# Turning q and k by halves, the order of a chunk's products, and seven PSUM banks dealt out anew, in a retention and feed-forward kernel

## Chip, cores and metric

One core of one Trainium2 chip. The metric is the device time of one execution in microseconds (us), as the median of several; lower is better.

## The reference

Retention (8 batches, 8 heads, 576 tokens, head size 64), then a feed-forward layer over all 4608 tokens with a squared ReLU. All in fp32.

```python
scores = scale * np.matmul(q, k.transpose(0, 1, 3, 2))
Dmat = np.where(rel >= 0, gamma[:, None, None] ** rel[None, :, :], 0.0)
attn = np.matmul(scores * Dmat, v)            # (B, H, S, D)
x = attn.transpose(0, 2, 1, 3).reshape(B * S, H * D)
h = np.maximum(x @ w_in, 0.0)                 # 512 -> 2048
return h * h @ w_out                          # 2048 -> 512
```

## The kernel before

Retention runs in 40 chunks (32 of 128 tokens, 8 of 64). One pass of the loop below, a *visit*, takes a chunk through one part of its work. Feed-forward steps of earlier tokens stand between the parts, so that TensorE has something to do while VectorE and ScalarE prepare the next part. The steps of block 0 (512 tokens) are plain products, L511 in the profile; from block 1 on a step is one of seven products of a Strassen scheme, L539. The second matrix of the layer comes last, L722.

For a chunk TensorE does this, in the profile's lines:

- *turn* of k and of q, L342: transposes by an identity matrix, since the scores need the head dimension on the partitions. ScalarE copies k out (L347), VectorE copies q out and applies a decay (L345).
- *scores*, L375: 64x64 products, read by VectorE with a mask into `ret` (L378).
- *a*, *b*, *c*, L392, L398 and L430: the retention output `x_ps` and the running state `u_ps`, all 64x64 products.

```python
ps_f = ctx.enter_context(tc.tile_pool(name="ps_f", bufs=4, space=PS))   # feed-forward
ps_a = first.enter_context(tc.tile_pool(name="ps_a", bufs=1, space=PS)) # turns
ps_x = first.enter_context(tc.tile_pool(name="ps_x", bufs=1, space=PS)) # x and scores, 2 banks
ps_u = first.enter_context(tc.tile_pool(name="ps_u", bufs=1, space=PS))
# ... cut ...
def turn(i, name):
    cs, c0 = chunks[i][3], chunks[i][2]
    src = loaded[i][name == "kT"]
    pool, tag = (ps_f, "f") if i < 6 else (ps_a, "a")
    p = pool.tile([128, HP, C], F32, tag=tag, name=f"{name}_ps")
    for hp in range(HP):
        nc.tensor.transpose(p[:, hp, :cs], src[:cs, 2 * hp:2 * hp + 2, :], ident[:cs, :cs])
    # ... cut: copy out by VectorE (q) or ScalarE (k) ...
# ... cut ...
for i in range(N_CH + 2):
    visit(i)                      # takes the two x banks
    if i >= 2:
        retain_a(i - 2)
    if i < N_CH:
        turn(i, "kT")
    # ... cut ...
    ffn(i - 2)                    # feed-forward steps that are due
    if i >= 2:
        retain_b(i - 2)
    if 1 <= i <= N_CH:
        scores(i - 1)
    if i < N_CH:
        turn(i, "qT")
    # ... cut ...
    ffn(i - 2)
    if i >= 2:
        # ... cut: steps that must come first ...
        retain_c(i - 2)
        convert(2 if i < 6 else 1)   # rounding of weights on VectorE
        ffn(i - 2)
    # ... cut ...
    if i + 2 < N_CH:
        load(i + 2)
```

## Time and profile before

| | |
|---|---|
| median of 3 | 1058.22 us (1057.21 to 1058.37) |
| TensorE busy in the profiled run | 996.0 us, 95% of the span of 1053.8 us |
| VectorE busy | 748.5 us, 71% |
| first feed-forward product | 55.4 us |
| first product of the last stage | 651.3 us |

What TensorE waits for, from its list of waits in the kernel before (us in total, times, longest):

```profile
PE kT_ps L342 <- DMA k_ld<-in_k_dram: 19.0, 6, 7.0
PE h_b L539 <- DVE room L475: 11.0, 3, 8.7
PE x_ps L392 <- ACT room L451: 8.3, 10, 1.2
PE x_ps L392 <- DVE ret L378: 6.8, 4, 4.6
PE x_ps L392 <- ACT w L451: 4.3, 4, 2.2
```

The first line is the start, which waits for loads of k. The second is feed-forward waiting for sums of its inputs on VectorE. The two `ACT` lines with L451 are waits for ScalarE's copy of the last chunk's output.

### The profile page before, as it was taken

What the parts mean: (1) busy time and instruction counts of PE and PEld (TensorE: products, weight loads), DVE (VectorE), ACT (ScalarE), POOL (GpSimd) and SP (SyncE); (2) the same over time, 40 slices, a digit from 0 to 9 for tenths busy, and PEclk for the clock granted to TensorE, in tenths of its full rate; (3) what the DMA queues carried; (4) which work ended last, traced back from release to release, by engine and by line L of the source; (5) the groups of instructions that cost most, each with busy time, mean ns of one, the idle gap of its engine ahead of it and who ended that gap; (6) DMA issues with size and microseconds to landing.
All of it is one profiled execution on the core that took longest, in us unless ns stands there. A gap on an engine that the chain in (4) does not pass through costs nothing.

```text
span 1053.8 us, 23361 instructions
## 1 busy us (share of the span) xinstructions
PE 996.0 (95%) x10120; PEld 876.6 (83%) x10120; DVE 748.5 (71%) x1414; ACT 184.7 (18%) x436; POOL 78.5 (7%) x82
## 2 busy tenths in 40 slices
PE   4699796999999999999999999899999999999998
PEld 3555455888888788888888888899999999999998
DVE  2377657776787878888887668667676677767775
ACT  2344321211122121221221100000000000000000
POOL 1111000111011010121110100000000000000000
PEclk9599898999999999999999999999999999999999
DMA  9969363744677788858956797954636546365351
GB/s 216 206 136 225 96 166 131 224 152 141 150 236 248 205 225 246 246 166 241 265 143 234 277 405 307 360 194 155 240 141 237 194 150 240 140 243 203 135 200 41
DMA packets 176342, 215.04 MB, mean 204 GB/s; under 512 B 115568, under 2 KB 124784, under 8 KB 167280
## 3 DMA queue, kind: packets, MB, share of 16 engines
q1 hardware_dynamic: 176240, 213.56, 64.5%
q8 instruction: 79, 1.29, 0.5%
q14 instruction: 23, 0.19, 0.1%
HBM read 125.19 MB, written 88.34 MB: 203 GB/s over the span
## 4 chain that ended last, share of the span: by engine, by line
PE 87%; DVE 5%; DMA 5%; ACT 1%; SPq 1%; issue 1%; DVEq 0%; ACTq 0%
PE h_b L539 16%; PE o_b L722 15%; PE h_c L539 10%; PE o_c L722 10%; PE o_a L722 10%; PE h_a L539 10%; PE h_ps L511 5%; DMA k_ld<-in_k_dram 3%; PE x_ps L392 3%; PE kT_ps L342 2%; PE x_ps L430 2%; PE qT_ps L342 2%; PE x_ps L375 1%; DMA a<-g_dram 1%; PE u_ps L398 1%
## 5 line engine op out<-in xcount | busy, mean ns | idle before, releaser
L539 PE MATMUL h_b<-room,w 128*128 128x256 f32 x736 | 177.4, 384 | 11.1 <-DVE room L475 11.0
L539 PEld LDWEIGHTS h_b<-room,w 128*128 128x128 f32 x736 | 138.0, 191 | 30.9 <-DVE room L475 12.0
L722 PE MATMUL o_b<-w,room 128*128 128x128 f32 x1168 | 144.5, 275 | 0.2 <-DVE room L694 0.2
L722 PEld LDWEIGHTS o_b<-w,room 128*128 128x128 f32 x1168 | 137.2, 192 | 0.5 <-DVE room L694 0.4
L722 PE MATMUL o_c<-w,room 128*128 128x128 f32 x1008 | 123.0, 275 | 0.0
L722 PEld LDWEIGHTS o_c<-w,room 128*128 128x128 f32 x1008 | 117.7, 192 | 0.0
L539 PE MATMUL h_c<-room,w 128*128 128x256 f32 x480 | 115.1, 383 | 0.0
L539 PE MATMUL h_a<-room,w 128*128 128x256 f32 x448 | 107.1, 382 | 0.0
L539 PEld LDWEIGHTS h_c<-room,w 128*128 128x128 f32 x480 | 90.2, 191 | 12.3
L539 PEld LDWEIGHTS h_a<-room,w 128*128 128x128 f32 x448 | 83.6, 190 | 11.8 <-issue 0.5
L722 PE MATMUL o_a<-w,a 128*128 128x128 f32 x688 | 85.9, 275 | 2.7 <-DMA a<-g_dram 2.7
L722 PEld LDWEIGHTS o_a<-w,a 128*128 128x128 f32 x688 | 81.3, 192 | 2.9 <-issue 2.9
L392 PEld LDWEIGHTS x_ps<-ret,v_ld 64*64 64x64 f32 x1152 | 44.5, 146 | 44.0 <-issue 33.3
L392 PE MATMUL x_ps<-ret,v_ld 64*64 64x64 f32 x1152 | 54.6, 238 | 20.0 <-ACT room L451 8.3
L546 DVE SCALAR_TENSOR_TENSOR room<-room 128x512 f32<-128x512 f32 x96 | 69.3, 722 | 3.3
L556 POOL TENSOR_TENSOR room<-room 128x512 f32<-128x512 f32 x32 | 34.6, 1081 | 471.2 <-ACT room L555 416.1
L733 ACT COPY r<-o_a 128x128 f32<-128x128 f32 x54 | 14.4, 266 | 276.9 <-PE o_a L722 236.1
L511 PE MATMUL h_ps<-room,w 128*128 128x512 f32 x128 | 60.2, 614 | 0.0
L558 DVE TENSOR_TENSOR room<-h_b,room 128x512 f32<-128x512 f32 x32 | 22.1, 691 | 46.5 <-PE h_b L539 46.5
L380 POOL TENSOR_TENSOR v_ld<-v_ld,dv 128x512 f32<-128x512 f32 (+1 forms) x40 | 43.5, 1090 | 97.7 <-DMA v_ld<-in_v_dram 87.0
L378 DVE TENSOR_TENSOR ret<-x_ps,msk 128x512 f32<-128x512 f32 (+1 forms) x40 | 27.4, 685 | 32.0 <-PE x_ps L375 26.5
L398 PE MATMUL u_ps<-v_ld,k_ld 64*64 64x64 f32 x1024 | 47.5, 237 | 0.0
(92 smaller groups left out, 1348.5 us busy)
## 6 DMA issues: line engine op xcount, KB each, us to landing
g_dram<-room SPq DMA_DIRECT2D x36, 1792.0 KB, 7.3
a<-g_dram SPq DMA_DIRECT2D x43, 1024.0 KB, 6.4
room<-g_dram SPq DMA_DIRECT2D x20, 1024.0 KB, 5.6
w<-w_dram SPq DMA_DIRECT2D x7, 1792.0 KB, 11.4
out_dram<-room SPq DMA_DIRECT2D x18, 512.0 KB, 3.3
q_ld<-in_q_dram SPq DMA_DIRECT2D x32, 256.0 KB, 5.8
k_ld<-in_k_dram SPq DMA_DIRECT2D x32, 256.0 KB, 6.4
v_ld<-in_v_dram SPq DMA_DIRECT2D x32, 256.0 KB, 6.8
```

Source lines behind the costliest of these rows:

```text
L342: nc.tensor.transpose(p[:, hp, :cs], src[:cs, 2 * hp:2 * hp + 2, :], ident[:cs, :cs])
L378: nc.vector.tensor_tensor(r[:cs], sc[:cs], msk[:cs].to_broadcast([cs, 2, HP, CH]), op=ALU.mult)
L380: nc.gpsimd.tensor_tensor(vs[:cs], vs[:cs], dv[:cs, :, ci:ci + 1].to_broadcast([cs, H, D]), op=ALU.mult)
L392: own.append(lambda g=g, e=e, b=b, head=head: nc.tensor.matmul(x_at(g, e, b, h), lhsT=s["vs"][rows(h), head, :], rhs=s["ret"][rows(h), e, ...
L398: grow.append(lambda hp=hp, e=e, head=head: nc.tensor.matmul(u_ps[0][rows(e), hp, :], lhsT=loaded[i][1][rows(1 - h), head, :], rhs=s["vs"] ...
L430: nc.tensor.matmul(x_at(g, e, b, h), lhsT=u[rows(e), 2 * b + g, :], rhs=s["qT"][rows(e), 2 * b + g, CH * h:CH * h + CH], start=clears(b, e ...
L511: nc.tensor.matmul(p.rearrange("p h t -> p (h t)"), lhsT=w[:, c, :], rhs=xT[0][:, c, :], start=(c == 0), stop=(c == N_DM - 1))
L539: nc.tensor.matmul(p[:, mm, :], lhsT=w[:, c, :], rhs=xs[n][right][:, c, :], start=(j in OPENS and mm == 0 and c == 0), stop=(j in CLOSES a ...
L546: nc.vector.scalar_tensor_tensor(t, t, 0.0, t, op0=ALU.max, op1=ALU.mult)
L556: nc.gpsimd.tensor_tensor(g["A11"], g["A11"], g["A11"], op=ALU.mult)
L558: nc.vector.tensor_tensor(g["A22"], p, p15, op=ALU.add)
L722: nc.tensor.matmul(p, lhsT=s["lefts"][left][:, m, :], rhs=w_out[j][:, m, WO_SLOT[right], :], start=(i in OPENS and m == 0), stop=(i in CLO ...
```

## The change

Its intent: make the transposes cheaper by running them in the two row halves of the array side by side, get q and k turned a visit earlier (one visit less of pipeline at the start), load three chunks ahead rather than two, and find the banks for it: turns and scores share two, x has two of its own, u has one, feed-forward keeps three of its four.

```diff
-    ps_f = ctx.enter_context(tc.tile_pool(name="ps_f", bufs=4, space=PS))
+    ps_f = ctx.enter_context(tc.tile_pool(name="ps_f", bufs=3, space=PS))
-    ps_a = first.enter_context(tc.tile_pool(name="ps_a", bufs=1, space=PS))
+    ps_t = first.enter_context(tc.tile_pool(name="ps_t", bufs=1, space=PS))
-    load(0)
-    load(1)
+    for i in range(3):
+        load(i)
 ... (old turn removed) ...
+    def turn(i):
+        cs, c0 = chunks[i][3], chunks[i][2]
+        n_h = cs // CH
+        p = ps_t.tile([128, 2, 512], F32, tag="t", name="t_ps").rearrange("p h (j d t) -> p h j d t", j=2, d=HP)
+        for j in (1, 0):
+            for hp in range(HP):
+                for h in range(n_h):
+                    nc.tensor.transpose(p[:, h, j, hp, :], loaded[i][j][rows(h), 2 * hp:2 * hp + 2, :],
+                                        ident[rows(h), rows(h)])
 ... (copies out by halves; kT in one buffer instead of two) ...
-        sc = xp[0][:, :, 256:].rearrange("p e (h t) -> p e h t", h=HP)
+        sc = ps_t.tile([128, 2, 512], F32, tag="t", name="sc_ps")[:, :, 0:256].rearrange("p e (h t) -> p e h t", h=HP)
 ... (main loop) ...
+    turn(0)
+    for i in range(N_CH + 1):
+        if i >= 1:
+            retain_a(i - 1)
+        convert(1 if i > 1 else 0)
+        ffn(i - 1)
+        if i >= 1:
+            retain_b(i - 1)
         if i < N_CH:
+            scores(i)
         convert(1 if i > 1 else 0)
+        ffn(i - 1)
+        if i + 1 < N_CH:
+            turn(i + 1)
 ... (steps that must come first) ...
+            retain_c(i - 1)
+        convert(2 if 1 <= i < 6 else min(i, 1))
+        ffn(i - 1)
 ...
-        if i + 2 < N_CH:
-            load(i + 2)
+        if i + 3 < N_CH:
+            load(i + 3)
-    ps_g = ctx.enter_context(tc.tile_pool(name="ps_g", bufs=4, space=PS))
+    ps_g = ctx.enter_context(tc.tile_pool(name="ps_g", bufs=5, space=PS))
```

In the profiles of the changed kernel the line numbers move: block 0's step is L514, the later steps L542, the turn L355, scores L376, `ret` L379, x L393, u L399, the b part L433.

More of the change, by code (lines that the diff above doesn't have):

```diff
@@ L333, in rows @@
         return slice(64 * half, 64 * half + n)
-    def turn(i, name):
-        cs, c0 = chunks[i][3], chunks[i][2]
-        src = loaded[i][name == "kT"]
-        pool, tag = (ps_f, "f") if i < 6 else (ps_a, "a")
-        p = pool.tile([128, HP, C], F32, tag=tag, name=f"{name}_ps")
-        for hp in range(HP):
-            nc.tensor.transpose(p[:, hp, :cs], src[:cs, 2 * hp:2 * hp + 2, :], ident[:cs, :cs])
-        t = st[i][name] = work2.tile([128, HP, C], F32, tag=name, name=name)
-        if name == "qT":
-            nc.vector.tensor_tensor(t[:, :, :cs], p[:, :, :cs], dq[:, :, c0:c0 + cs], op=ALU.mult)
-        else:
-            nc.scalar.copy(t[:, :, :cs], p[:, :, :cs])
     xp = [None]
     clean = set()
-    def visit(i):
-        xp[0] = ps_x.tile([128, 2, 512], F32, tag="x", name="x_ps")
-        clean.clear()
     def clears(half, bank):
@@ L363, in clears @@
         return new
+    def turn(i):
[7 more added lines that the diff above has]
+                                        ident[rows(h), rows(h)])
+        for j, name in ((1, "kT"), (0, "qT")):
+            t = st[i][name] = work2.tile([128, HP, C], F32, tag=name, name=name) if j == 0 else work.tile([128, HP, C], F32, tag=name, name=name)
+            to = t[:, :, :cs].rearrange("p d (h t) -> p h d t", h=n_h)
+            if j:
+                nc.scalar.copy(to, p[:, :n_h, j, :, :])
+            else:
+                nc.vector.tensor_tensor(to, p[:, :n_h, j, :, :], dq[:, :, c0:c0 + cs].rearrange("p d (h t) -> p h d t", h=n_h),
+                                        op=ALU.mult)
     def scores(i):
@@ L375, in scores @@
                     nc.tensor.matmul(sc[rows(h), e, hp, :], lhsT=kT[rows(e), hp, t], rhs=qT[rows(e), hp, t],
-                                     start=clears(h, e), stop=True, skip_group_check=True)
+                                     start=True, stop=True, skip_group_check=True)
         r = st[i]["ret"] = work2.tile([128, 2, HP, CH], F32, tag="ret", name="ret")
@@ L408, in retain_a @@
         b_, ci, c0, cs = chunks[i]
+        xp[0] = ps_x.tile([128, 2, 256], F32, tag="x", name="x_ps", padded_shape=[128, 2, 512])
+        clean.clear()
         if ci == 0:
@@ L438, in retain_c @@
         more = ci + 1 < NCH
-        if i == N_CH - 1:
-            nc.scalar.copy(u_sb[(2 * ci + 1) % 3][:, 0:2, 0:1], xp[0][:, :, 0:1])
+        if i >= N_CH - 2:
+            nc.scalar.copy(u_sb[(2 * ci + (cs // CH)) % 3][:, 0:2, 0:1], xp[0][:, :, 0:1])
         for j in range(0, len(own), 2):
@@ L616 @@
     n_late = [5]
-    for i in range(N_CH + 2):
-        visit(i)
-        if i >= 2:
-            retain_a(i - 2)
+    turn(0)
[6 more added lines that the diff above has]
+            retain_b(i - 1)
         if i < N_CH:
-            turn(i, "kT")
-        elif steps:
-            step()
+            scores(i)
         convert(1 if i > 1 else 0)
-        ffn(i - 2)
-        if i >= 2:
-            retain_b(i - 2)
-        if 1 <= i <= N_CH:
-            scores(i - 1)
-        if i < N_CH:
-            turn(i, "qT")
-        elif steps:
-            step()
-        convert(1 if i > 1 else 0)
-        ffn(i - 2)
-        if i >= 2:
-            b, ci, c0, cs = chunks[i - 2]
+        ffn(i - 1)
+        if i + 1 < N_CH:
+            turn(i + 1)
+        if i >= 1:
+            b, ci, c0, cs = chunks[i - 1]
             n = (b * S + c0 + cs - 1) // TOK
@@ L643 @@
                 step()
-            retain_c(i - 2)
-            convert(2 if i < 6 else 1)
-            ffn(i - 2)
+            retain_c(i - 1)
+        convert(2 if 1 <= i < 6 else min(i, 1))
+        ffn(i - 1)
+        if i >= 1:
             while n_next[0] < N_BLK and (n_next[0] + 1) * TOK <= b * S + c0 + cs:
@@ L702, in bank @@
         n_bank[0] += 1
-        pool, tag = ((ps_f, "f"), (ps_g, "g"))[(n_bank[0] // 4) % 2]
+        pool, tag = (ps_f, "f") if n_bank[0] % 8 < 3 else (ps_g, "g")
         return pool.tile([128, 512], F32, tag=tag, name=name)[:, 0:128]
```

## The prediction

> **What bounds the kernel now.** I read the page first (engine shares and the 40 slices), then busy time by stretch, then TensorE's timeline at the start and in a steady visit, then what TensorE waits for. A visit is one pass of the loop over the 40 chunks of retention (32 chunks of 128 tokens, 8 of 64), with feed-forward steps put between its products.
>
> The busy time by stretch (PE, PEld, DVE, ACT, POOL, then granted clock, DMA share, GB/s):
>
> ```profile
> 0.00:60.00 60.00, 36.73 (x675) 28.69 (x676) 21.09 (x37) 17.39 (x34) 9.99 (x18) 0.74 1.00 198
> 60.00:180.00 120.00, 99.66 (x1203) 60.34 (x1201) 80.42 (x151) 39.02 (x89) 9.35 (x8) 0.91 0.65 159
> 180.00:660.00 480.00, 473.27 (x4791) 401.62 (x4790) 373.37 (x613) 95.58 (x191) 59.13 (x56) 1.00 0.72 227
> 660.00:1054.00 394.00, 386.30 (x3458) 385.95 (x3456) 273.67 (x616) 32.76 (x123) 0.00 (x0) 1.00 0.51 191
> ```
>
> The first 60 us are bound by loads (DMA share 1.00, TensorE idle for 23.3 us of them, at 0.74 of its clock). From 60 to 180 us TensorE idles 20.3 us, in waits on VectorE and short gaps. From 180 us to the end TensorE is the bound: it idles 6.7 us of 480, then 7.7 us of 394. The change touches the stages up to 660 us; of the last stage it alters only which pool a bank comes from, with eight in turn as before.
>
> The end of the load-bound start, in the timeline of TensorE:
>
> ```profile
> 50.80 1.12 PE L342 MATMUL kT_ps<-ident,k_ld 128*128 128x128 f32 x4 [4.30 <-DMA k_ld<-in_k_dram]
> ...
> 54.38 1.12 PE L392 MATMUL x_ps<-ret,v_ld 64*64 64x64 f32 x16
> 55.43 3.70 PE L511 MATMUL h_ps<-room,w 128*128 128x512 f32 x8
> ```
>
> The first feed-forward product (55.43) comes after the load of chunk 6's keys (50.80) and 4.6 us of products. Until it starts, TensorE has no filler.
>
> A steady visit, in the same view, later:
>
> ```profile
> 202.90 0.68 PE L392 MATMUL x_ps<-ret,v_ld 64*64 64x64 f32 x16
> 203.51 1.99 PE L539 MATMUL h_b<-room,w 128*128 128x256 f32 x8
> ...
> 207.16 0.27 PE L392 MATMUL x_ps<-ret,v_ld 64*64 64x64 f32 x2
> ...
> 207.79 0.66 PE L342 MATMUL kT_ps<-ident,k_ld 128*128 128x128 f32 x4
> 208.28 1.89 PE L539 MATMUL h_b<-room,w 128*128 128x256 f32 x8
> ...
> 217.87 0.66 PE L342 MATMUL qT_ps<-ident,q_ld 128*128 128x128 f32 x4
> 218.36 1.89 PE L539 MATMUL h_b<-room,w 128*128 128x256 f32 x8
> ```
>
> Ends of matmuls are modelled, so I count from start to start. Turning k takes 207.79 to 208.28 = 0.49 us, turning q 217.87 to 218.36 = 0.49 us.
>
> **What the Trainium skill says.** (1) "TensorE: Matmul & The Clock Gate", Part 3, "The mechanism": a weight load runs beside matmuls in flight where its row group differs. This trace agrees for the 64x64 form: sixteen instructions, all in one row half, take 202.90 to 203.51 = 0.61 us; thirty-two, half of them in each row half, take 207.16 to 207.79 = 0.63 us. (2) "TensorEngine Tiling (Array Packing)", "Key Properties": changing the tiling mode drains TensorE. The trace agrees: about 0.1 us a change, below. (3) "PSUM — Partial Sum Buffer", "PSUM bank collisions raise a hardware error": guard by bank and quadrant, not address. The trace shows such a guard costing time:
>
> ```profile
> 110.52 1.12 PE L392 MATMUL x_ps<-ret,v_ld 64*64 64x64 f32 x16 [4.63 <-DVE ret L378]
> ```
>
> The output columns of that product are not those that L378 reads; only the two banks are the same. (4) "TensorE: Matmul & The Clock Gate", Part 1: the clock halves after idle time. The trace agrees: 0.74 in the first 60 us, 1.00 from 180 us.
>
> **The change, part by part.**
>
> *Turning by halves.* For a full chunk, eight 128x128 transposes (four of k, four of q) become sixteen of 64 rows by 128 columns with 64 moving columns, alternating between row halves and between two banks. The old kernel has that form in its short chunks, in one half only:
>
> ```profile
> L342 PE MATMUL kT_ps<-ident,k_ld 64*128 64x64 f32 x32 | 3.9, 246 | 1.5 <-DMA k_ld<-in_k_dram 1.5
> ```
>
> ```profile
> 263.33 0.46 PE L342 MATMUL kT_ps<-ident,k_ld 64*128 64x64 f32 x4
> 263.72 1.99 PE L539 MATMUL h_b<-room,w 128*128 128x256 f32 x8
> ```
>
> Four that lie 0.46 us from first start to last end, each 0.246 us long, have a pitch of (0.46 - 0.246) / 3 = 0.071 us. The four hold TensorE for 0.39 us, of which 4 x 0.071 = 0.28 is work and 0.11 the extra mode change. If the two halves run side by side, sixteen cost eight pitches: 0.57 us.
>
> *Order.* Both turns now stand together, in the visit before, directly ahead of the last group of retention products. By the built order a visit had three runs of small matmuls between feed-forward steps, with six mode changes; it still has three, with seven. So turning costs 0.57 + 0.11 = 0.68 us a chunk, full or short (a short chunk's eight are all in one half, eight pitches too). Before: 0.49 + 0.49 = 0.98 for a full chunk, 0.39 + 0.39 = 0.78 for a short one. Saved: 0.30 and 0.10. Where filler has begun TensorE is the bound and this counts in full; that is so for the turns of chunks 7 to 39, about 26 full and 7 short: 26 x 0.30 + 7 x 0.10 = 8.5 us.
>
> *Loads one chunk further ahead, one visit less of pipeline.* Up to chunk 6's keys the queue carried chunks 0 to 5 (4224 KB), the decay tables (1172 KB), sixteen half pieces of weights (4096 KB) and chunk 6's q and k (512 KB): 10004 KB by 50.8 us, 197 KB per us. The new order has twelve half pieces ahead of them, 8980 KB: 45.6 us, an estimate at the same rate. After that the old kernel needed 4.6 us to the first feed-forward product. The new one needs the turn of chunk 6 (the cold short turn took 34.47 to 35.09 = 0.62 us for four, so 1.24 for eight pitches) and the products at 54.38, 1.05 us: first product near 48, against 55.4. The work left at that point is the same, so 7.4 us come off.
>
> *What it adds.* Scores now share their banks with the turns, one buffer, so the next turn waits until VectorE has read the scores. Before, the retention products waited for that same read, so the wait of 4.63 us moves rather than goes. Taking the end of that read from the old trace and the number of feed-forward steps between: only the visits with one step of 1.7 us between are too short, some 0.1 to 0.7 us each in perhaps five visits, and at 110 us the turn (0.7 to 1.2 us) can no longer hide in the wait. I put 2.5 us. The built program also makes VectorE's q copy wait for ScalarE's k copy, about 0.8 us a visit (0.59 us copy and a handover). VectorE is busy 78% from 180 to 660 us, so mostly absorbed; I allow 2 us.
>
> *Three feed-forward banks for four.* The tightest reuse is the b sum: closed in the seventh step, opened again two steps on. Comparing, in the old trace, the end of VectorE's last read with the start of the matmul that would reuse its bank, all 31 cases have it free, the tightest by 0.43 us, most by 0.8 us or more. 0 us by itself; it removes slack.
>
> Sum: 1058.2 - 8.5 - 7.4 + 2.5 + 2 = 1046.8, say **1046.5 us**, 1.1% less.
>
> **Rivals.** *The halves do not overlap.* Then sixteen turns cost 16 x 0.071 + 0.11 = 1.25 us, 0.27 more than before: 26 x 0.27 = 7 us lost instead of 8 gained, and the time is about 1061. For it: no transpose in this trace runs in two halves at once. Against: matmuls do. One in eight. *VectorE or the banks take the gain back.* With q's copy behind k's and three banks, a late read of b stops TensorE: a few tenths in each of the 31 reuses, up to 10 us, time about 1055. For it: VectorE is busy over 80% in parts of 300 to 420 us. Against: most margins are 0.8 us and over. *More comes off than I sum.* If the waits of 60 to 180 us (4.63 us at 110, 8.7 us at 166 before L475's sums) also shrink with the new alignment, and the clock stays up with them, 8 to 10 us more: about 1037. I see no reason in the order of the instructions: L475's sums follow the same chain on VectorE. *The start is hidden.* If weights rather than chunks hold the start, since their pieces come later now, the 7.4 us shrink to 2 or 3: about 1051.
>
> **Range and chances.** The centre is the sum; the low end has the early waits shrink, the high end has the start's gain lost and some bank stalls. 1036 to 1056. Over 2% faster means below 1037.1: 0.12. Over 2% slower means above 1079.4, worse than every rival: 0.02. Within 2%: 0.86.
>
> **What would show it.** Right: a full chunk's turn of sixteen instructions taking 0.55 to 0.7 us start to start, against 0.98; the first feed-forward product near 48 us; TensorE idle from 180 to 660 us still under 10 us; no wait of h_b on L565's read. Wrong: a pitch of 0.07 us for each transpose rather than each pair; the first feed-forward product after 52 us; turns waiting for the scores' read by more than 5 us in total beyond the first 60 us; the 4.6 and 8.7 us waits gone.

## More of the kernel before

The page's slices say what clock TensorE was granted, in tenths of full speed; each digit is 26 us:

```profile
PEclk9599898999999999999999999999999999999999
```

The second digit says half speed from 26 to 53 us.

## The result

The changed kernel took 1056.18 us (median of 4, 1054.76 to 1056.61), against 1057.86 for the kernel before (4 runs). The ratio is 0.9982, 95% interval 0.9965 to 0.9999: the same within 2%. A ratio here is the mean of one kernel's runs over the mean of the other's from the same rounds, so not quite the ratio of the medians quoted. Run again with the first experiments it was 1056.0 against 1057.32, ratio 0.9992 (0.9977 to 1.0007). The profiled runs differ by 0.8 us. So the change is worth about one or two microseconds (the second interval takes in none at all), where I had expected 11.7, and 1056.18 lies just above my range.

Busy time by stretch, of the kernel after (same columns as in the prediction):

```profile
0.00:60.00 60.00, 35.64 (x770) 28.48 (x771) 21.88 (x38) 17.70 (x34) 9.99 (x18) 1.00 1.03 209
60.00:180.00 120.00, 99.30 (x1199) 58.43 (x1198) 79.52 (x149) 38.50 (x87) 9.72 (x8) 0.90 0.61 153
180.00:660.00 480.00, 469.48 (x4953) 396.63 (x4952) 374.88 (x613) 96.33 (x193) 59.09 (x56) 1.00 0.72 227
...
```

TensorE is busy 3.8 us less from 180 to 660 us, yet that stretch did not end sooner: it idles 10.5 us there instead of 6.7. Busy time that falls while the span stays is either waiting or work that was not on the path; here the ends of matmuls are modelled too, so I went over to starts.

The moments that cut the run into stages (start of the first instruction, us; FF stands for feed-forward) tell where the time went:

| | first FF product | block 1's first step | first product of the last stage | end |
|---|---|---|---|---|
| before | 55.43 | 155.95 | 651.33 | 1053.83 |
| after | 52.07 | 155.17 | 650.57 | 1053.05 |
| after is ahead by | 3.36 | 0.78 | 0.76 | 0.78 |

Two things are to be explained: a lead of 3.4 us at the start that melts to 0.8 by 155 us, and a long middle in which nothing is gained.

**The start.** The timeline of TensorE in the kernel after:

```profile
27.49 1.08 PE L376 MATMUL sc_ps<-qT,kT 64*64 64x64 f32 x32
29.38 0.69 PE L355 MATMUL t_ps<-ident,k_ld 64*128 64x64 f32 x8 [0.81 <-DVE ret L379]
...
32.32 0.48 PE L393 MATMUL x_ps<-ret,v_ld 64*64 64x64 f32 x4 [0.76 <-ACT room L454]
...
34.15 1.13 PE L433 MATMUL x_ps<-qT,u_sb 64*64 64x64 f32 x32 [0.53 <-ACT u_sb L405]
35.06 1.08 PE L376 MATMUL sc_ps<-qT,kT 64*64 64x64 f32 x32
...
52.07 5.38 PE L514 MATMUL h_ps<-room,w 128*128 128x512 f32 x8
...
88.72 0.33 PE L393 MATMUL x_ps<-ret,v_ld 64*64 64x64 f32 x4 [1.82 <-ACT room L454]
...
89.51 5.40 PE L514 MATMUL h_ps<-room,w 128*128 128x512 f32 x8
```

The last wait of the start that TensorE's list puts down to a load ended at 13.60 us. The wait of 3.70 us that ended at 26.58 still goes back to one: TensorE waited for ScalarE's copy, this stood behind ScalarE's part in rounding a piece of weights, and VectorE had begun that rounding at 24.49, after waiting for the piece's load:

```profile
24.49 0.43 DVE L206 TENSOR_SCALAR w<-w 128x512 uint32<-128x512 uint32 x1 [3.33 <-DMA w<-in_moe_w_in_dram]
26.58 1.13 PE L433 MATMUL x_ps<-qT,u_sb 64*64 64x64 f32 x32 [3.70 <-ACT u_sb L405]
```

From 26.6 us to the first feed-forward product no wait is put down to a load. A visit lasts 35.06 - 27.49 = 7.57 us, as a chain: scores, then a wait for VectorE's `ret`, turn and c, a wait for ScalarE's copy, a, another wait, b, the next scores. And TensorE runs this chain at half speed: thirty-two score products are listed with 1.08 us, where the same line has 0.65 later; inside the step at 52.07 the second to fourth products start 0.85 us apart (by the start times in the trace), the last ones 0.429. The granted clock of the first stretch reads 1.00. Record and durations contradict each other; I go by the durations.

**The lead melts at half-speed steps.** The same stretch in the kernel before:

```profile
89.81 0.33 PE L392 MATMUL x_ps<-ret,v_ld 64*64 64x64 f32 x4 [1.16 <-ACT room L451]
...
91.10 3.60 PE L511 MATMUL h_ps<-room,w 128*128 128x512 f32 x8
```

There the wait was 1.16 us and the step after it ran at full speed, 3.6 us. After, the wait is 1.82 and the step takes 5.4. That costs 1.8 us; the first step (5.38 against the 3.70 that the prediction shows at 55.43) costs 1.7. The lead goes 3.36 at step 0, 2.23 at step 1, 1.59 at step 6, 0.28 at step 7. One profile each would be little to go by. Step 6 was slow in all seven profiles of kernels with the new order, three groups and no added products (after, c0, e1, e2, e3, e6, e8: 4.99 to 5.40 us), and fast in all three of kernels with the old one (before, e5, e11: 3.60). Step 0 was slow in the same seven, but also in one of the three: e11, the kernel before up to that point, took 6.03 us. So the loss at step 6 belongs to the change, and that at step 0 is partly chance.

The wait alone does not sort the steps; the stretch without feed-forward products, small products and waits together, does it better. Counted from one pitch (0.43 us) after the last start of a step to the first start of the next, it is 3.24 us ahead of step 6 before the change and 4.04 after. In nine profiles without added products in block 0 (those above but for e11, which adds some) every step from 1 to 15 ran fast after at most 3.39 us and slow after 3.80 us or more. In e4, with other groups, steps ran fast up to 4.20 us, so this is a sorting of what was seen and no limit.

**The middle.** A steady visit of the kernel after, in the timeline (a full chunk):

```profile
201.95 0.46 PE L355 MATMUL t_ps<-ident,k_ld 64*128 64x64 f32 x8
202.25 0.41 PE L355 MATMUL t_ps<-ident,q_ld 64*128 64x64 f32 x8
202.59 0.68 PE L393 MATMUL x_ps<-ret,v_ld 64*64 64x64 f32 x16
203.20 1.99 PE L542 MATMUL h_b<-room,w 128*128 128x256 f32 x8
205.03 1.89 PE L542 MATMUL h_c<-room,w 128*128 128x256 f32 x8
```

The turn of a full chunk takes 202.59 - 201.95 = 0.64 us, against 0.98 before and 0.68 predicted. But look at the step after: it is listed with 1.99 us and the next starts 1.83 later. In the prediction's lines from the kernel before, the steps at 208.28 and 218.36, which follow a 128x128 turn, have 1.89 (next start 1.73 later); the one at 203.51, after 64x64 products, has 1.99. From the start times: the first to the eighth product of a step take 1.513 us (median) where the step follows a 128x128 turn (39 cases before), 1.615 where it follows anything with 64 rows (36 cases before, all 72 after), and 1.511 inside a stretch of steps. So 0.10 us is the price of going from 64 rows to 128, and it is paid by the step. That it is the rows and not the turn, e7, e9 and e10 below show: behind added 128x128 products (step 0 of e7, step 8 of e9 and e10) the seven pitches of a block 0 step take 3.01 us, behind 64 rows 3.11. Before, two of a visit's three steps after small products stood behind a turn, and the turn had already paid.

The waits of TensorE after:

```profile
PE h_b L542 <- DVE room L478: 13.6, 4, 8.7
PE t_ps L355 <- DMA k_ld<-in_k_dram: 9.9, 2, 6.9
PE t_ps L355 <- DVE ret L379: 9.9, 8, 4.5
PE x_ps L393 <- ACT room L454: 8.6, 10, 1.8
PE x_ps L433 <- ACT u_sb L405: 6.7, 6, 3.7
```

The load wait is halved. The last line is new: it is the start's wait behind the weights (3.70) and five shorter ones. The wait for `ret` now stands before turns (4.49 us of it at 109.86, where before 4.63 stood in front of x). The sums (L478, the old L475) have one wait more:

```profile
603.87 1.97 PE L542 MATMUL h_b<-room,w 128*128 128x256 f32 x8 [1.80 <-DVE room L478]
```

Before, the last chunk's products (with 0.43 us of wait) lay at this place, and the second step found its sums ready:

```profile
601.92 0.68 PE L392 MATMUL x_ps<-ret,v_ld 64*64 64x64 f32 x16 [0.43 <-ACT u_sb L441]
...
604.63 1.97 PE L539 MATMUL h_b<-room,w 128*128 128x256 f32 x8
```

Between block 1's first step and the last stage, start to start: the small products cost 91.0 us beyond the steps before and 85.2 after, 5.8 less. What the feed-forward steps take beyond 1.73 us each rose from 17.7 to 23.4, 5.8 more: 3.5 in first steps, 2.5 in waits, -0.2 elsewhere. The middle lasts 495.38 before and 495.40 after.

### The profile page after: what moved, and what is told of

Its sections match the earlier page's. It is cut to its first block, busy times and chain, and to the rows that moved or that the text cites. A ratio compares the mean times of both kernels' runs of the same rounds, so it can differ in the third digit from the quotient of the medians.

```text
span 1053.1 us, 23813 instructions
## 1 busy us (share of the span) xinstructions
PE 991.0 (94%) x10376; PEld 869.8 (83%) x10376; DVE 749.9 (71%) x1414; ACT 185.3 (18%) x437; POOL 78.8 (7%) x82
## 4 chain that ended last, share of the span: by engine, by line
PE 87%; DVE 6%; DMA 2%; ACT 2%; SPq 1%; issue 1%; ACTq 0%; DVEq 0%
PE h_b L542 16%; PE o_b L720 15%; PE h_c L542 11%; PE o_c L720 10%; PE o_a L720 10%; PE h_a L542 10%; PE h_ps L514 5%; PE x_ps L393 3%; PE t_ps L355 2%; PE x_ps L433 2%; PE sc_ps L376 2%; DMA a<-g_dram 1%; PE u_ps L399 1%; DVE room L549 1%; DMA k_ld<-in_k_dram 1%
## 5 line engine op out<-in xcount | busy, mean ns | idle before, releaser
L542 PE MATMUL h_b<-room,w 128*128 128x256 f32 x736 | 179.1, 387 | 13.6 <-DVE room L478 13.6
L542 PEld LDWEIGHTS h_b<-room,w 128*128 128x128 f32 x736 | 138.0, 191 | 34.7 <-DVE room L478 9.3
L542 PE MATMUL h_c<-room,w 128*128 128x256 f32 x480 | 116.6, 386 | 0.0
L542 PE MATMUL h_a<-room,w 128*128 128x256 f32 x448 | 107.8, 383 | 0.0
L542 PEld LDWEIGHTS h_c<-room,w 128*128 128x128 f32 x480 | 90.5, 192 | 13.2
L542 PEld LDWEIGHTS h_a<-room,w 128*128 128x128 f32 x448 | 83.5, 190 | 12.3 <-issue 0.5
L393 PE MATMUL x_ps<-ret,v_ld 64*64 64x64 f32 x1152 | 54.9, 239 | 12.7 <-ACT room L454 8.6
L514 PE MATMUL h_ps<-room,w 128*128 128x512 f32 x128 | 65.6, 660 | 0.0
L393 PEld LDWEIGHTS x_ps<-ret,v_ld 64*64 64x64 f32 x1152 | 44.6, 147 | 24.7 <-issue 19.8
L514 PEld LDWEIGHTS h_ps<-room,w 128*128 128x128 f32 x128 | 25.4, 210 | 28.2 <-issue 27.0
L399 PE MATMUL u_ps<-v_ld,k_ld 64*64 64x64 f32 x1024 | 47.8, 238 | 0.0
```

Source lines behind the costliest of these rows:

```text
L393: own.append(lambda g=g, e=e, b=b, head=head: nc.tensor.matmul(x_at(g, e, b, h), lhsT=s["vs"][rows(h), head, :], rhs=s["ret"][rows(h), e, ...
L399: grow.append(lambda hp=hp, e=e, head=head: nc.tensor.matmul(u_ps[0][rows(e), hp, :], lhsT=loaded[i][1][rows(1 - h), head, :], rhs=s["vs"] ...
L514: nc.tensor.matmul(p.rearrange("p h t -> p (h t)"), lhsT=w[:, c, :], rhs=xT[0][:, c, :], start=(c == 0), stop=(c == N_DM - 1))
L542: nc.tensor.matmul(p[:, mm, :], lhsT=w[:, c, :], rhs=xs[n][right][:, c, :], start=(j in OPENS and mm == 0 and c == 0), stop=(j in CLOSES a ...
```

## The experiments

Each ran beside the kernel before on the same chip. All outputs are right. "After" is the changed kernel. It ran again only in the first of three sessions (c0, with e1, e3 and e4), so the others are compared with it by their ratios to before.

| | what | median us | ratio to before (95%) |
|---|---|---|---|
| c0_after | after, again | 1056.0 | 0.9992 (0.9977 to 1.0007) |
| e1_whole | turn by whole 128x128 | 1064.87 | 1.0065 (1.0037 to 1.0094) |
| e3_split | a step between turn and c | 1068.1 | 1.0106 (1.0088 to 1.0124) |
| e4_merge | two groups of small products, not three | 1065.45 | 1.0082 (1.0059 to 1.0106) |
| e2_load2 | loads two ahead | 1060.92 | 1.0046 (1.0029 to 1.0064) |
| e5_bank3 | before with three FF banks | 1055.14 | 0.9997 (0.9978 to 1.0017) |
| e7_warm | many products in the start's waits | 1053.85 | 0.9978 (0.996 to 0.9996) |
| e8_last | last visit in another order | 1055.09 | 0.9994 (0.9975 to 1.0013) |
| e6_row | halves one after the other | 1057.67 | 1.0013 (0.9996 to 1.003) |
| e9_warm2 | few products in the waits | 1046.98 | 0.9912 (0.9896 to 0.9929) |
| e10_fill | e9, e8 and two more waits filled | 1044.83 | 0.9895 (0.9876 to 0.9914) |
| e11_bfill | before, two waits filled | 1053.07 | 0.9965 (0.9943 to 0.9988) |

### e1_whole: what is turning by halves worth in itself?

```diff
-            for hp in range(HP):
-                for h in range(n_h):
-                    nc.tensor.transpose(p[:, h, j, hp, :], loaded[i][j][rows(h), ...], ident[rows(h), rows(h)])
+            for hp in range(HP):
+                nc.tensor.transpose(p[:, j, hp, :cs], loaded[i][j][:cs, ...], ident[:cs, :cs])
```

> The changed kernel with whole 128x128 transposes (k into one bank, q into the other) in place of the halves; order, loads and banks as changed. Theory A (the halves do overlap and shorten the path, but the mode changes that turns used to absorb are now paid by the feed-forward steps): a full chunk's turn takes about 0.90 us start to start in place of 0.64, so from 180 to 660 us TensorE loses about 20 x 0.26 = 5 us and the whole is 5 to 8 us slower than the changed kernel. Theory B (turning was not on the path; VectorE and the banks ate the gain): within 2 us of the changed kernel, or faster, since q's copy no longer waits for k's.

The group of turn and c takes 1.81 us instead of 1.58, so the halves save 0.23 us a full chunk where nothing else differs. The middle is 4.4 us longer (499.83 against 495.40), as 20 full chunks at 0.23 make 4.6. Another 5.6 us were lost before block 1 (first step at 160.77): 1.3 by the first product, 1.2 in half-speed steps even longer than those of after, and 2.4 ahead of steps 6 and 9, where the waits grew from 1.8 to 2.4 and from 4.5 to 5.1 us. In all e1 is 8.9 us slower than after by the medians, just over the 5 to 8 expected. The halves do their work.

### e6_row: do the halves run side by side?

```diff
-            for hp in range(HP):
-                for h in range(n_h):
+            for h in range(n_h):
+                for hp in range(HP):
```

> The changed kernel with the eight transposes of a turn's k (and of its q) in another order: all of one row half, then all of the other, in place of alternating. Same instructions, same banks. Theory A (a pair costs one pitch because the two row halves run beside each other): without alternation each transpose costs about 0.07 us, a full chunk's turn about 1.2 us in place of 0.64, and from the first step of block 1 to the last stage about 21 x 0.55 = 11 us more; 1066 to 1070 us. If the halves never overlapped: no change.

I expected that four transposes of one half in a row would queue up, and a loss of about 11 us. The middle is unchanged (495.06; block 1 starts at 158.18, 3.0 us later than in after, after longer waits and half-speed steps), and a turn is 0.05 us dearer:

```profile
203.74 0.47 PE L355 MATMUL t_ps<-ident,k_ld 64*128 64x64 f32 x8
...
204.43 0.68 PE L393 MATMUL x_ps<-ret,v_ld 64*64 64x64 f32 x16
```

That looks like a refutation of "side by side", and it is not one. Three counts settle it. The prediction's four transposes of one half in the kernel before (263.33) start 0.062 us apart, as the start times in the trace say. In after, *eight* in one half (the short chunks) take 0.642 us start to start and *sixteen* in two halves 0.641: the second half is free. And the single starts of after come in pairs 0.003 us apart, pair after pair 0.062. In e6_row most come in pairs too, 0.007 to 0.015 apart, pair after pair 0.062, although the program, as built too, has four of one half first. One in-order queue does not explain that: four of one half alone start 0.062 apart. It looks as if the array took up the other half's transposes while those of the first were still waiting. The trace does not name the half of a record, so this last step is an inference from the starts and is not shown. My expectation failed because I took the order in the program for the order in the array.

### e5_bank3: do three feed-forward banks cost anything?

```diff
 (in the kernel before)
-    ps_f = ... bufs=4
+    ps_f = ... bufs=3
-    ps_g = ... bufs=4
+    ps_g = ... bufs=5
```

> The kernel before with three feed-forward banks for four (five for four in the last stage), nothing else. Theory A: no difference, 0.998 to 1.002, and no wait of TensorE on the read of a feed-forward bank. Theory B (banks ate the gain): 0.3% or more slower.

Ratio 0.9997, the middle 495.33 against 495.38. Nothing was lost to the banks, as the margins in the trace had said.

### e3_split and e4_merge: is it the number of groups?

If each group of small products costs the steps around it, more groups must cost and fewer save. e3 puts a feed-forward step between turn and c; e4 makes two groups of three.

```diff
 e3_split
             turn(i + 1)
+            if steps and steps[0][0] > 0:
+                owed[0] -= 1
+                step()
```

> The changed kernel with one feed-forward step moved between each turn and the retention products that follow it, once steps of block 1 on exist: one more run of small matmuls per visit, about 26 visits. The steps and products are the same in number. Theory A (each run of small matmuls costs about 0.1 us on entry and 0.1 us inside the first feed-forward step after it): 0.2 us a visit, 4 to 6 us slower than the changed kernel, and first feed-forward steps after a run take 1.83 us to the next, the others 1.73. Theory B: no difference beyond 1 us, perhaps a little faster as VectorE and ScalarE get time to copy.

```diff
 e4_merge: order [a, scores] step step [b, fence, turn, c]
-        ffn(i - 1)
-        if i >= 1:
-            retain_b(i - 1)
         if i < N_CH:
             scores(i)
         convert(1 if i > 1 else 0)
         ffn(i - 1)
+        convert(1 if i > 1 else 0)
+        ffn(i - 1)
+            retain_b(i - 1)
+            fence(i - 1)      # a small ScalarE copy that reads b's bank
         turn(i + 1)
```

> The changed kernel with the small products in two runs a visit in place of three: first part of retention and the scores, feed-forward, then second part, turn and third part (with a tiny ScalarE copy that orders the two writers of the x banks). Theory A: one run less saves about 0.2 us a visit, 5 to 8 us faster than the changed kernel, about 1049. Theory B: no gain, or slower where the longer run waits for copies, 1055 to 1060.

e3 went the expected way and further: 91 groups in the middle for 72, and the middle 10 us longer. The groups take 4.8 us more, of which 3.9 are waits (6.8 us instead of 2.9 for ScalarE's copy of x); the feed-forward steps take 5.2 more, of which 3.5 are first steps: 19 more of them at 0.10 make 2.0, and one step at half speed (535.82) makes 1.6. So of the 10 us the price of the entries explains 2; the rest is mostly waits and the slow step. e4 missed. It has 49 groups for 72 and an early first product, 48.71 us, but the middle is 10.8 us longer. The fence, which the two writers of one bank needed between them, is why:

```profile
PE x_ps L393 <- ACT u_sb L441: 15.2, 12, 3.5
```

With b, turn and c in one group TensorE has nothing to put over ScalarE's copy; 15.2 us of new waits (9.2 of them in the middle) ate what the groups saved. The middle group is there for a reason: it separates products that wait for each other. So e4 says nothing against the price of a group; whether it can be saved where no wait comes back, no run here shows.

### e2_load2: did the loads or the order bring the start forward?

```diff
-    for i in range(3):
+    for i in range(2):
         load(i)
-        if i + 3 < N_CH:
-            load(i + 3)
+        if i + 2 < N_CH:
+            load(i + 2)
```

> The changed kernel with loads two chunks ahead in place of three. Theory C: the earlier loads are what brought the first feed-forward product from 55.4 to 52.1 us; without them it falls back to 55 us or later. What of it reaches the end: if the lead is lost to slow-clock steps by 100 us anyway, within 2 us of the changed kernel; if it is kept, 3 to 4 us slower.

First product at 53.48, where I had expected no earlier than 55. Of the 3.4 us of lead, then, about 2 come from the order and 1.4 from the loads, give or take the 0.5 by which after and c0 differ (52.07 and 52.54). The total is worse than expected: waits for loads of k rise again (17.6 us in five for 9.9 in two; one of 4.44 us ends at 51.39, just before the first product), 3.2 us of them in the middle, which lasts 499.30, 4 us longer. The test is harsher than it looks. The turns stand a visit earlier, so that two ahead leaves no whole visit between a load and its turn; the kernel before had one, and after has one. So e2 is no return to the loads of before.

### e8_last: the wait at 603.87

```diff
         convert(1 if i > 1 else 0)
-        ffn(i - 1)
+        if i < N_CH:
+            ffn(i - 1)
```

> The changed kernel without the feed-forward call between the second and third part of the last chunk's retention, so that these come one after the other and before more of block 7's steps. Theory A: the last block's input sums start while block 7 still has steps, the wait of 1.8 us on L478 before block 8's second step goes, one run of small products less: about 2 us faster than the changed kernel. If the wait is due to VectorE being behind: no change.

The waits for L478 fall from 13.6 to 13.1 us only (the one in question from 1.80 to 1.28, where about 2 us off were expected) and the middle from 495.40 to 495.14; the total cannot be told from after's. Skipping one call of steps in the last visit does not undo the loss. It stays small in any case.

### e7_warm and e9_warm2: is it the clock?

The rule that I wanted to test: a step after waits runs at half speed because TensorE was too idle just before. The Trainium skill, "TensorE: Matmul & The Clock Gate", Part 1, "What's actually happening", says that the clock goes by how busy the array was in a window of 3.4 us. Products of the identity matrix with itself, into a bank that nobody reads, put into the waits should then make later steps fast without touching the data. `warm(n)` issues n of them (the trace counts two instructions for each).

```diff
+    def warm(n):
+        p = ps_f.tile([128, 2, HT], F32, tag="f", name="warm_ps").rearrange("p h t -> p (h t)")
+        for _ in range(n):
+            nc.tensor.matmul(p[:, 0:128], lhsT=ident[:, :], rhs=ident[:, :], start=True, stop=True, skip_group_check=True)
 e7_warm: in visits 0 to 5, warm(4) after scores, warm(4) after c, warm(3) after a
```

> The changed kernel with idle-time transposes-sized products (3 or 4 128x128 products of the identity, into a feed-forward bank that nobody reads) after each group of small products in the first six visits, to keep TensorE's clock up while the start waits for copies. Theory C (after 26 us the start is no longer bound by loads but by a chain of products at half speed and copies, 7.5 us a visit; half of that is products): the scores' 32 instructions take about 0.6 us in place of 1.0, the first feed-forward product comes at 47 to 50 us in place of 52.1, and its first step takes 3.6 us in place of 5.3; 3 to 6 us less at the first step of block 1. Theory D (loads bind the start as before): first feed-forward product still at 51 us or later, as the added products only fill waits.

Step 0 took 3.60 us, as expected. But the first product came at 51.21, later than the 47 to 50 expected: visits shrank from 7.57 to 6.3 us, but the wait behind the weights was 5.39 us long (to 27.95) for 3.70. That much of Theory D was right. The lead held until step 5 (2.6 us over after) and went at step 6, which still took over 6 us: no products had been added there. At block 1 e7 stands where after stands (155.12).

```diff
 e9_warm2: fewer in the first six visits, and some where step 6 needs them
+            if i < 6: warm(1)              # after a
+        if i < 6: warm(2)                  # after scores
+        if i < 5: warm(2)                  # after c
+        left = len(steps)
         ffn(i - 1)
+        if 6 <= i < 16 and len(steps) == left:
+            warm(3)                        # no step was due: fill the wait
```

> The changed kernel with fewer added products in the first six visits than in e7_warm (2, 2 and 1 in place of 4, 4 and 3) and three more wherever, up to visit 15, the last part of a chunk's retention is followed by the first part of the next with no feed-forward step between. Theory E (the lead won at the start is lost at the seventh feed-forward step, whose matmuls run at half speed after a wait of 1.8 us): the seventh step takes 3.6 us in place of 5.1 to 5.3, the first feed-forward product comes before 50 us, and the first step of block 1 comes 2 to 5 us earlier, at 150 to 153 us; total 1051 to 1054. Theory F (VectorE's and ScalarE's chain of weight rounding sets the time at 110 us whatever TensorE does): first step of block 1 within 0.7 us of 155.2, total as the changed kernel.

```profile
83.59 0.94 PE L622 MATMUL warm_ps<-ident 128*128 128x128 f32 x6
85.96 0.33 PE L393 MATMUL x_ps<-ret,v_ld 64*64 64x64 f32 x4 [1.43 <-ACT room L454]
...
86.75 3.70 PE L514 MATMUL h_ps<-room,w 128*128 128x512 f32 x8
```

Step 6 at full speed, 3.70 for 5.40 us, with a wait still in front of it. Step 0 too (50.51, 3.70). Block 1 starts at 150.10, 5.1 us before after, and that lead is kept to the end: 1046.98 us, less than the 1051 expected at best. Theory F, that a chain through VectorE fixes the start of block 1 whatever TensorE does, fails with this: that chain's wait for `ret`, at 109.86 in after, ended at 106.52. It is not without force: the lead was 4.5 us at step 7 and 2.3 at step 9, and faster steps 9 and 11 (4.20 for 5.38 us, 3.70 for 5.09) brought it back. This agrees with the skill's rule that the array's recent work sets its clock: with three identity products in the wait the step took 3.70 us for 5.40. The length of the window no run here shows. The gain is one of the clock.

### e10_fill and e11_bfill: the other waits

```diff
 e10_fill: e9 and e8, and
+        if i == 10: warm(16)                       # in the 4.5 us wait for ret
+        if (n, mp, j) == (1, 0, 1): warm(30)       # in the 8.7 us wait for the sums
 e11_bfill: the same two in the kernel before (warm(16) ahead of retain_c at i == 11)
```

> e9_warm2 with the change of e8_last, sixteen added products in the wait for the scores' read at 105 to 110 us and thirty in the wait before block 1's second step (157 to 166 us), so that the steps after these waits run at full speed. Theory E and F alike: the tenth step takes 3.6 us in place of 5.1 and block 1's second step 1.8 us in place of 3.6, 3 to 4 us off the changed kernel from these alone, 1049 to 1053 with e9_warm2's gain where there is one.

> The kernel before with the same sixteen and thirty added products in its own two waits (at 105 to 110 us and at 157 to 166 us), nothing else. Slow-clock steps after waits cost it the same there: 2 to 4 us faster than before, 1053 to 1055. If it gains as much as e10_fill does, the change itself is no part of that gain.

After the long wait for the sums the step took 3.78 us in before and in after. With the wait filled, e10:

```profile
147.64 6.86 PE L624 MATMUL warm_ps<-ident 128*128 128x128 f32 x60
156.60 1.97 PE L544 MATMUL h_b<-room,w 128*128 128x256 f32 x8 [2.10 <-DVE room L478]
```

The step starts when it would have started anyway and takes half as long. e11 gains 2.4 us in the middle (492.97) and 0.35% in all, in the kernel without the change; that comes from this second wait. Its sixteen products in the first wait brought nothing: the step at 115.27 took 4.87 us, against 4.94 in before. e10 is the fastest kernel here: 1044.83, 1.05% less than before. Its step 9 took the 3.70 us expected, but its step 6 fell back to 5.40 in the profiled run, with the same three identity products ahead of it as in e9 (the wait behind them 1.59 us for 1.43). So that fill works in one profile of two. A few idle products do not do it everywhere.

## Why the prediction was wrong

Turning by halves, the banks and the moved wait were right in mechanism; the sum was not. Term by term (middle: block 1's first step to the last stage; of the 26 full and 7 short turns, 20 and 5 lie in it, 6.5 us of the 8.5 predicted):

| term | predicted | measured |
|---|---|---|
| start | -7.4 | -3.4 at the first product, -0.8 at block 1 |
| turns, in the middle | -6.5 | -5.8 in the small products |
| the steps behind them | none | +3.5 |
| new waits | +2.5 and +2 | +2.5 in the middle, at the sums |

- **Turning by halves: right in mechanism.** Sixteen in 0.64 us for 0.68 predicted (a pitch of 0.062 for the 0.071 that I had worked out), the halves side by side (e6's counts, e1's 0.23 us).
- **First failed step: "turning costs 0.57 + 0.11 = 0.68 us a chunk ... Before: 0.49 + 0.49 = 0.98 ... Saved: 0.30".** I counted the extra mode change for the turn but not whom it had served before. A 128x128 turn behind 64x64 products held the change to 128 rows within its own 0.49 us and gave the next step a full-speed entry. With it gone the step pays 0.10, two times a full chunk: 0.98 - 0.64 - 0.20 = 0.14 us saved, not 0.30. Twenty full chunks make 2.8 and five short ones, where the old step had paid too, 5 x 0.14 = 0.7. Measured net, 5.8 - 3.5 = 2.2; 1.1 of the difference is a longer wait for `ret` in the middle (1.4 us in front of turns for 0.3 in front of x). The prediction's own lines had it: 1.99 at 203.51 and 1.89 at 208.28.
- **Second failed step: "first product near 48, against 55.4 ... so 7.4 us come off".** The loads of k did move out of the way: TensorE waits for none after 13.60 us, where before it still did at 50.80. But I put nothing in their place. A half-speed chain with 2.1 us of waits in every visit took over, 7.57 us each, and the first product came at 52.07. Of the rivals, "the start is hidden" has the right size, and its reason, the weights, is part of it: 3.70 us of wait to 26.58 go back to a piece of weights. The chain's speed is the other part: in e10, with that wait (3.91 us) still there and idle products in the others, the first product came at 47.81 (50.51 in e9, the same program up to there, with a pause of 2.42 us that its trace doesn't explain).
- **The same step again, "the work left at that point is the same".** The work is, its speed is not. Half-speed steps at 52.07 and 89.51 gave 3.5 us away; e9 took them back with a few idle products. That the clock follows the waits was in my text, as a remark on the granted clock, and was not put into the sum.
- **Third failed step: the new waits.** I allowed 2.5 us for turns behind the scores' read and 2 for VectorE's q copy behind k's. In the middle 2.5 us did come, from elsewhere: the sums of block 8's inputs, probably since the last chunk's products no longer lie in front of them (e8 put that only partly to the test). Behind the scores' read the turns waited 9.9 us in all, where x had waited 6.8. q's copy does wait for k's (28.8 us of VectorE's time in 18 waits), but TensorE waited for q's copy only once, 1.4 us at 9.37.
- **Right:** three banks cost nothing (e5); the wait of 4.63 us moved (4.49 at 109.86) and did not go; the wait for the sums stayed at 8.71. Three of the prediction's own signs spoke against it: the first product after 52 us, turns waiting 5.9 us for the scores' read beyond 60 us (it allowed 5), and TensorE idle for 10.5 us from 180 to 660 (it allowed 10).

With the true sizes, -0.8 at block 1, -2.2 net in turns and +2.5 in waits, the sum is -0.5, against -0.8 in the profiled runs. What exactly made step 6 slow stays open: a stretch of 3.24 us with a wait of 1.16 was harmless, 4.04 with 1.82 was not, and with six identity instructions in it the step was fast once (e9) and slow once (e10).

## What to carry to other kernels

When you take a group of instructions out from between two others, ask what the next one gets for free from it: here a step's entry from 64 rows to 128. When a load stops binding, work out the chain that binds next, with the durations of the cold stage. And look at the step after each wait: if it takes nearly twice its usual time, a few throwaway products in the wait can be worth more than the change itself: 9 us less than before for both together here (e9), against 1 or 2 for the change alone. They can also do nothing, as at the first wait of e11.

## What the Trainium skill lacked or had wrong

- "TensorEngine Tiling (Array Packing)", "Key Properties", says that changing the mode drains TensorE and gives no cost. Here a step of eight fp32 products has its first seven pitches in 1.615 us after a group with 64 rows, 1.513 after 128x128 work: 0.10 us, and it falls on the work that follows.
- "TensorE: Matmul & The Clock Gate", Part 3, "The mechanism", has matmuls start strictly in program order. In e6_row most transposes start in pairs 0.007 to 0.015 us apart although the program has four of one half before four of the other; that the pairs are of both halves, against that order, is inferred from the starts and not shown. No page has what fp32 transposes by halves cost: pairs at 0.062 us, sixteen in two halves 0.641 us, eight in one half 0.642.
- The same page, Part 1, has full speed lost after an idle window of some 3.4 us. Here 1.82 us of waiting, amid small 64x64 products, was followed by a step at half speed (5.40 us for 3.70), and six identity instructions mended it in one profile of two. So small products and waits count together: in nine profiles stretches up to 3.39 us without feed-forward products were harmless and those from 3.80 us on were not, which is near the page's window.
- The same page's caveat that clock records are unreliable holds: the granted clock of the first 60 us is 1.00 after the change while score products took 1.08 us for 0.65, and 0.74 before it.
